# Transposing q and k of a batch with one DMA each, and keeping queries and keys in the same 128-token blocks

## The chip, the core and the metric

The kernel runs on one NeuronCore of one Trainium2 chip. A core has a matrix engine (TensorE, PE in the profile; its weight loads are PEld), a vector engine (VectorE, DVE), a scalar engine (ScalarE, ACT), GpSimd (POOL) and a sync engine (SyncE, SP). POOL and SP are used here mostly to issue DMAs: POOL the loads, which also convert float32 to bfloat16, and SP the transposing DMAs, the stores and a small round trip through DRAM. The transfers of both run on the core's 16 DMA engines. The metric is the device time of one execution in microseconds; lower is better.

## The reference

A sliding-window attention with a distance bias, and behind it a gated feed-forward block. Batch 8, 8 heads, 576 tokens of a sequence, head size 64; the feed-forward block sees 4608 tokens of width 512 and has 1536 hidden channels.

```python
scores = scale * np.matmul(q, k.transpose(0, 1, 3, 2))
rel = pos[:, None] - pos[None, :]
bias = slopes[:, None, None] * (-np.abs(rel).astype(np.float32))[None, :, :]
mask = (rel >= 0) & (rel < 128)
scores = np.where(mask, scores + bias[None], -1000000000.0)
attn = np.exp(scores - np.max(scores, axis=-1, keepdims=True))
attn = attn / (np.sum(attn, axis=-1, keepdims=True) + 1e-09)
x = np.matmul(attn, v)            # then (batch, token, head * 64): 4608 x 512
g, val = x @ w_gate, x @ w_val
out = (0.5 * g * (1.0 + erf(g * inv_sqrt2)) * val) @ w_out
```

## The kernel before

**Attention.** Scores are kept transposed: keys on the partitions, queries along the free dimension. With a window of 128 and keys in blocks of 128, a key block meets at most two blocks of queries, so a head has five score matmuls (`score`, line 130). Key blocks are shifted by 64 tokens: block j holds the keys 128j - 64 to 128j + 63, and the first 64 columns of block 0 are zero padding. Query ranges start at `Q0` and are `NQ` wide: 192, 256, 256, 256 and 128 columns. ScalarE takes the exponential out of PSUM into the tile P (`exp`, line 137), VectorE multiplies with a precomputed mask that holds the bias and the window (`mask`, line 140; the masks `emask` and `emask2` are made once by `masks`). `PCOL` says at which columns of P each key block lies.

Scores need q and k with the head dimension on the partitions. Two heads (a pair c, 0 to 3) share 128 partitions. For batch 0 TensorE transposes them (`transposes`, line 111, through PSUM, and a copy by VectorE, line 116). For all later batches SP issues transposing DMAs (`transposes_dma`, line 122): for one half u of the heads (u = 0: pairs 0 and 1, u = 1: pairs 2 and 3) five for k and five for q, one for each 128 tokens (the fifth has 64), each over 256 columns, that is two blocks of 128 by 128. A batch has twenty of them. `qT` and `kT` exist twice and are used by turns.

**Loads.** `load_qk(b, u)` (line 84) loads half the heads of q and k of a batch with ten DMAs from POOL into slabs `qsb` and `ksb`, which have two buffers each; a slab is free for the next half when its transposes have read it. `load_v(b)` (line 93) loads v in five DMAs with all heads; `load_w` and line 280 load the weights.

**Sums and values.** `sums(b)` (line 191) adds the masked exponentials of all heads with a matmul of ones, VectorE takes the reciprocals (lines 198 and 199), and SP sends them to DRAM (`rd`, line 203) and back as a tile that is spread over all partitions (`rb`, line 205). `values(b, c)` (line 216) is the product with v, and VectorE multiplies by `rb` on the way to `xT` (line 222).

**Feed-forward.** Nine groups g of 512 tokens. `gate_val(g, f)` (line 235) makes a block of 128 hidden channels: eight matmuls, Gelu on ScalarE (line 239), product on VectorE (line 240). `out_half(g, u)` (line 250) is half of the output product of 128 tokens; after every second one ScalarE copies (line 255) and SP stores (line 257).

**Order.** The order of instructions on each engine is the order of the program (a manual schedule): an instruction that waits holds everything behind it on its engine or queue. Ahead of the main loop: loads of batch 0, then of batch 1's first half, v, weights, batch 1's second half; transposes and all eight score steps of batch 0; the transposing DMAs of batch 1's first half; `sums(0)`; the first four score steps of batch 1; `values(0, c)`. Then for each group g: loads and transposing DMAs of a coming batch (group 0: batch 1's second half and batch 2's first; group 1: the rest of batch 2 and batch 3; group g from 2 on: batch g + 2), `load_v(g + 2)`, all of `gate_val` (from group 2 on with `values(g + 1, c)` between), and then score steps and output halves by turns: eight score steps, in group 1 twelve. A batch has eight steps, two for each pair c; from group 2 on they are those of batch g + 2, from pair 0 to pair 3. SP meets the transposing DMAs of a group ahead of that group's stores.

Of the kernel before, what the change touches and what calls it, by code (L numbers as in the profile page):

```python
# [7 lines left out]
FP32 = mybir.dt.float32  # L8
BF16 = mybir.dt.bfloat16
# [5 lines left out]

NQ = (192, 256, 256, 256, 128)
Q0 = (0, 64, 192, 320, 448)

PCOL = (768, 0, 256, 512, 960)
# [5 lines left out]
def kernel(  # L25
# [10 lines left out]
    nc = tc.nc  # L36
    B, H, S, D = q.shape
    W = 128
    NTOK = B * S
    DM = H * D  # L40
# [8 lines left out]
    slab = ctx.enter_context(tc.tile_pool(name="slab", bufs=2))  # L49
# [25 lines left out]
    slabs = {}  # L75

    def load_qk(b, u):

        for nm, src in (("qsb", q), ("ksb", k)):
            t = slab.tile([128, 5, DM // 2], BF16, name=nm)  # L80
            slabs[nm, b, u] = t
            for j in range(5):
                sz = min(128, S - 128 * j)
                nc.gpsimd.dma_start(  # L84
                    out=t[0:sz, j, :].rearrange("p (h d) -> p h d", h=H // 2),
                    in_=src[b][4 * u:4 * u + 4, 128 * j:128 * j + sz, :].rearrange("h p d -> p h d"),
                )

    def load_v(b):
        t = vb[b % 2]  # L90
        for j in range(5):
            lo = 64 if j == 0 else 0
            nc.gpsimd.dma_start(  # L93
                out=t[lo:128, j, :].rearrange("p (h d) -> p h d", h=H),
                in_=v[b][:, 128 * j - 64 + lo:128 * j + 64, :].rearrange("h p d -> p h d"),
            )
# [7 lines left out]
    def transposes(b, c):  # L104
        for nm in ("qsb", "ksb"):
            src = slabs[nm, b, c // 2]
            ps = bank().bitcast(BF16)
            lo = 128 * (c % 2)
            for j in range(5):
                sz = min(128, S - 128 * j)  # L110
                nc.tensor.transpose(
                    out=ps[:, 128 * j:128 * j + sz],
                    in_=src[0:sz, j, lo:lo + 128],
                    identity=ident[0:sz, 0:sz])
            dst = qT[b % 2][:, c, :] if nm == "qsb" else kT[b % 2][:, c, 64:64 + S]
            nc.vector.tensor_copy(out=dst, in_=ps[:, 0:S])

    def transposes_dma(b, u):
        for nm, dst, off in (("ksb", kT[b % 2], 64), ("qsb", qT[b % 2], 0)):
            for j in range(5):  # L120
                sz = min(128, S - 128 * j)
                nc.sync.dma_start_transpose(
                    out=dst[:, 2 * u:2 * u + 2, off + 128 * j:off + 128 * j + sz],
                    in_=slabs[nm, b, u][0:sz, j, :])
# [3 lines left out]
    def score(b, c, i, j, ps, col):  # L128
        lo = 64 * i
        nc.tensor.matmul(  # L130
            out=ps[:, col:col + NQ[j]],
            lhsT=kT[b % 2][lo:lo + 64, c, 128 * j:128 * j + 128],
            rhs=qT[b % 2][lo:lo + 64, c, Q0[j]:Q0[j] + NQ[j]],
            start=True, stop=True)

    def exp(dst, src):
        nc.scalar.activation(out=dst, in_=src, func=AF.Exp, scale=0.125)  # L137
# [26 lines left out]
    def scores2(b, c):  # L164
        P = probs[b, c - c % 2][:, c % 2]
        ps = [bank(), bank()]
        for j in (0, 3):
            for i in (0, 1):
                score(b, c, i, j, ps[i], PCOL[j] - 512)
# [74 lines left out]
    def out_half(g, u):  # L244
# [16 lines left out]
    load_qk(0, 0)  # L261
    relt = consts.tile([128, 256], mybir.dt.int32, name="relt")
    tmpl = consts.tile([128, 256], FP32, name="tmpl")
    nc.gpsimd.affine_select(
        out=ident, in_=ident, compare_op=ALU.not_equal, fill=1.0,
        base=0, pattern=[[-1, 128]], channel_multiplier=1)
    nc.gpsimd.iota(relt, pattern=[[1, 256]], base=0, channel_multiplier=-1)
# [5 lines left out]
    load_qk(0, 1)  # L273
    load_qk(1, 0)
    load_v(0)
    step = DFF // 4
    for n in range(4):
        load_w(step * n, step * (n + 1))
    load_qk(1, 1)
    nc.gpsimd.dma_start(out=wo, in_=moe_w_out.rearrange("(c p) f -> p c f", p=128))  # L280
    load_v(1)
    for i in range(2):
        nc.vector.memset(kT[i][:, :, 0:64], 0.0)
        nc.vector.memset(vb[i][0:64, 0, :], 0.0)
# [4 lines left out]
    nc.vector.memset(emask2[0:64, :, 256:448], 0.0)  # L289

    def masks(c):
# [4 lines left out]
        nc.vector.tensor_copy(out=e2[:, :, 0:256], in_=e)  # L296
        nc.vector.tensor_copy(out=e2[64:128, :, 256:448], in_=e[64:128, :, 64:256])
# [24 lines left out]
    transposes_dma(1, 0)  # L322
# [73 lines left out]
```

## Time and profile before

| | |
|---|---|
| median of 3 runs | 456.78 us (454.81 to 457.54) |
| profiled execution | 456.34 us |
| its span, first to last instruction | 454.6 us |
| TensorE busy (weight loads beside it) | 368.8 us, 81% (167.0 us) |
| VectorE, ScalarE, GpSimd busy | 184.4, 176.3, 157.6 us |
| mean granted TensorE clock | 0.935 |
| DMA packets, bytes | 166000, 46.61 MB, 151568 of them under 512 B |
| DMA queue of POOL's loads | 119568 packets, 18.89 MB, 57.8% of 16 engines' span |
| DMA queue of SP | 46400 packets, 27.30 MB, 26.4% |

Times in rows of the profile count from the start of the span. A row of the timeline has start, length, engine, line, operation, output and inputs with shapes, how many instructions are merged in it, and in brackets how long the engine had been idle before it and what ended that. SPq is SP's queue of DMA issues: the length is the time that SP spends on issuing, not that of the transfer. "Landing" is the time from the issue to the end of the transfer. A row of the windows has the window, its length, the busy time of each engine with its number of instructions, the granted clock, the share of time in which the DMA engines were busy (it can be above 1, since transfers of several queues overlap) and GB/s.

### The profile page before, as it was taken

The page shows a single profiled execution, that of the slowest core. Times are in us where ns is not written, and L with a number is a line of the kernel's source. Part 1 is how long each engine was busy: PE and PEld are TensorE (multiplying, and loading weights), DVE is VectorE, ACT ScalarE, POOL GpSimd, SP SyncE. Part 2 cuts the span into 40 slices and gives each one's busy share as a digit, 9 for nine tenths or more (in the row PEclk, how much of TensorE's full clock was granted, in tenths as well). Part 3 has the DMA queues.
Part 4 walks back from the last instruction along what each step waited for, and adds up shares of the span by engine and source line. Part 5 has one row for each costly group of instructions (what it writes and reads, how often), then busy time and mean ns, then how long its engine had stood idle before and what let it go on. Part 6 is the DMA issues. An engine that isn't in the chain of part 4 may idle for free. (4 is left out here: it accounts for less than half of the span.)

```text
span 454.6 us, 6481 instructions
## 1 busy us (share of the span) xinstructions
PE 368.8 (81%) x2424; PEld 167.0 (37%) x2424; DVE 184.4 (41%) x281; ACT 176.3 (39%) x326; POOL 157.6 (35%) x218
## 2 busy tenths in 40 slices
PE   2631399749978569969995999689968999999996
PEld 1220234314434134423442344234423444444442
DVE  2481344615345074434453355325542651230330
ACT  1350423524364314364435442544254422332321
POOL 8993173951095640249024900681000000000000
PEclk9999889859997689998999799989997999999999
DMA  8999999999199999499949994999521321101002
GB/s 52 78 128 174 228 139 161 132 146 176 41 96 125 133 169 163 62 105 128 162 65 106 118 125 96 97 126 142 96 47 71 80 50 48 46 0 71 24 1 93
DMA packets 166000, 46.61 MB, mean 103 GB/s; under 512 B 151568, under 2 KB 157200, under 8 KB 165968
## 3 DMA queue, kind: packets, MB, share of 16 engines
q0 software_dynamic: 119568, 18.89, 57.8%
q1 hardware_dynamic: 46400, 27.30, 26.4%
q8 instruction: 19, 0.31, 0.3%
q14 instruction: 13, 0.11, 0.1%
HBM read 47.19 MB, written 9.58 MB: 125 GB/s over the span
## 5 line engine op out<-in xcount | busy, mean ns | idle before, releaser
L240 DVE TENSOR_TENSOR hT<-ps,gelu 128x512 bf16<-128x512 f32 x108 | 74.7, 691 | 124.2 <-PE ps L235 124.1
L235 PE MATMUL ps<-xT,wg 128*128 128x512 bf16 x432 | 112.4, 382 | 7.8 <-DVE xT L222 7.4
L250 PE MATMUL ps<-wo,hT 128*128 128x512 bf16 x432 | 115.1, 416 | 0.1
L239 ACT ACTIVATE gelu<-ps 128x512 bf16<-128x512 f32 x108 | 64.5, 597 | 126.3 <-PE ps L235 125.9
L235 PE MATMUL ps<-xT,wv 128*128 128x512 bf16 x432 | 111.6, 381 | 0.0
L84 POOL DMA_DIRECT2D qsb<-in_q_dram x80 | 58.0, 754 | 131.5 <-DMA qT<-qsb 113.2
L137 ACT ACTIVATE P<-ps 128x512 bf16<-128x512 f32 (+2 forms) x160 | 72.9, 553 | 69.1 <-PE ps L130 69.0
L140 DVE TENSOR_TENSOR P<-P,emask 128x1024 bf16<-128x1024 bf16 x64 | 46.1, 724 | 88.1 <-ACT P L137 88.1
L130 PE MATMUL ps<-qT,kT 64*128 64x256 bf16 (+2 forms) x320 | 29.6, 304 | 45.4 <-DMA qT<-qsb 42.6
L84 POOL DMA_DIRECT2D ksb<-in_k_dram x80 | 58.3, 781 | 18.4 <-DMA qsb<-in_q_dram 9.3
L235 PEld LDWEIGHTS <-wg 128*128 128x128 bf16 x432 | 41.1, 98 | 58.1 <-issue 8.9
L250 PEld LDWEIGHTS <-hT 128*128 128x128 bf16 x432 | 41.3, 104 | 57.4 <-issue 22.5
L235 PEld LDWEIGHTS <-wv 128*128 128x128 bf16 x432 | 42.4, 98 | 52.0 <-issue 1.5
L255 ACT COPY osb<-ps 128x512 f32<-128x512 f32 x36 | 21.2, 588 | 69.8 <-PE ps L250 52.4
L130 PEld LDWEIGHTS <-kT 64*128 64x128 bf16 x320 | 12.9, 105 | 68.2 <-issue 56.5
L222 DVE TENSOR_TENSOR xT<-ps,rb 128x320 bf16<-128x320 f32 x64 | 25.4, 449 | 24.7 <-DMA rb<-rd 23.7
L93 POOL DMA_DIRECT2D vb<-in_v_dram x40 | 34.2, 933 | 0.5 <-DMA qsb<-in_q_dram 0.5
L191 PE MATMUL ps<-P,ones 128*32 128x128 bf16 (+2 forms) x384 | 14.5, 281 | 13.9 <-DVE P L140 13.7
L216 PE MATMUL ps<-P,vb 128*64 128x128 bf16 (+2 forms) x384 | 20.8, 248 | 1.4 <-DVE xT L222 1.4
L198 DVE RECIPROCAL r<-ps 128x320 f32<-128x320 f32 x8 | 17.3, 2157 | 6.2 <-PE ps L191 6.2
L216 PEld LDWEIGHTS <-vb 128*64 128x64 bf16 x384 | 15.0, 111 | 11.9 <-issue 11.7
L191 PEld LDWEIGHTS <-ones 128*32 128x32 bf16 x384 | 10.9, 111 | 18.5 <-issue 18.2
(31 smaller groups left out, 68.8 us busy)
## 6 DMA issues: line engine op xcount, KB each, us to landing
rb<-rd SPq DMA_DIRECT2D x16, 576.0 KB, 6.0
out_dram<-osb SPq DMA_DIRECT2D x36, 256.0 KB, 2.7
qsb<-in_q_dram POOLq DMA_DIRECT2D x64, 64.0 KB, 3.2
ksb<-in_k_dram POOLq DMA_DIRECT2D x64, 64.0 KB, 3.5
vb<-in_v_dram POOLq DMA_DIRECT2D x32, 128.0 KB, 5.0
wg<-in_moe_w_gate_dram POOLq DMA_DIRECT2D x4, 384.0 KB, 12.9
wv<-in_moe_w_val_dram POOLq DMA_DIRECT2D x4, 384.0 KB, 14.3
wo<-in_moe_w_out_dram POOLq DMA_DIRECT2D x1, 1536.0 KB, 14.3
```

The costliest lines, as they stand in the source:

```text
L84: nc.gpsimd.dma_start(out=t[0:sz, j, :].rearrange("p (h d) -> p h d", h=H // 2), in_=src[b][4 * u:4 * u + 4, 128 * j:128 * j + sz, :].rear ...
L93: nc.gpsimd.dma_start(out=t[lo:128, j, :].rearrange("p (h d) -> p h d", h=H), in_=v[b][:, 128 * j - 64 + lo:128 * j + 64, :].rearrange("h ...
L130: nc.tensor.matmul(out=ps[:, col:col + NQ[j]], lhsT=kT[b % 2][lo:lo + 64, c, 128 * j:128 * j + 128], rhs=qT[b % 2][lo:lo + 64, c, Q0[j]:Q0 ...
L137: nc.scalar.activation(out=dst, in_=src, func=AF.Exp, scale=0.125)
L140: nc.vector.tensor_tensor(out=dst, in0=dst, in1=m, op=ALU.mult)
L191: nc.tensor.matmul(out=ps[s][32 * c:32 * c + 32, a - QS * s:e - QS * s], lhsT=ones[:, i, :], rhs=probs[b, c - c % 2][:, c % 2, i, col:col ...
L216: nc.tensor.matmul(out=ps[s][64 * i:64 * i + 64, a - QS * s:e - QS * s], lhsT=vb[b % 2][:, j, 64 * h:64 * h + 64], rhs=P[:, i, col:col + e ...
L222: nc.vector.tensor_tensor(out=xT[:, c, b * S + lo:b * S + hi], in0=ps[s][:, 0:hi - lo], in1=recip[b][:, c, lo:hi], op=ALU.mult)
L235: nc.tensor.matmul(out=ps, lhsT=w[:, c, 128 * f:128 * (f + 1)], rhs=xT[:, c, t0:t0 + 512], start=(c == 0), stop=(c == 3))
L239: nc.scalar.activation(out=gl, in_=pg, func=AF.Gelu)
L240: nc.vector.tensor_tensor(out=hid[g][:, f, :], in0=pv, in1=gl, op=ALU.mult)
L250: nc.tensor.matmul(out=po, lhsT=hid[g][:, f, 128 * t:128 * (t + 1)], rhs=wo[:, f, :], start=(f == 0), stop=(f == NF - 1))
```

## The change

q and k of a batch are loaded whole, all eight heads in five DMAs each, in the same shifted token blocks as v (the first block holds 64 tokens, its other 64 rows are zero), into one buffer `qs` and one `ks`. Each is then transposed by one DMA over all of its 20 blocks of 128 by 128, instead of ten. `qT` and `kT` get the form (block, pair, token). Because queries now lie in the same blocks as keys, key block j is scored against the query blocks j and j + 1; block 0 scores 256 columns instead of 192, the first 64 of which are padding that the exponential leaves out. The columns of P and the masks move accordingly.

The order changes too. Batch 0 is loaded whole at once, after the identity is made. The loads of batch 1, v and the weights stand behind the score steps of batch 0 in the program, and batch 1 is loaded and transposed whole there. In the loop, group g loads and transposes batch g + 2, in groups 0 and 1 as in all others.

```diff
-PCOL = (768, 0, 256, 512, 960)
+PCOL = (512, 0, 256, 704, 960)
...
-    slab = ctx.enter_context(tc.tile_pool(name="slab", bufs=2))
...
-    qT = [consts.tile([128, 4, S], BF16, name=f"qT{i}") for i in range(2)]
-    kT = [consts.tile([128, 4, 64 + S], BF16, name=f"kT{i}") for i in range(2)]
+    qs, ks = (consts.tile([128, 5, DM], BF16, name=f"{nm}s") for nm in "qk")
+    qT, kT = ([consts.tile([128, 5, 4, 128], BF16, name=f"{nm}T{i}") for i in range(2)]
+              for nm in "qk")
...
-    def load_v(b):
-        t = vb[b % 2]
+    def load(t, src, b):
         for j in range(5):
             lo = 64 if j == 0 else 0
             nc.gpsimd.dma_start(
                 out=t[lo:128, j, :].rearrange("p (h d) -> p h d", h=H),
...
+    def load_qk(b):
+        load(qs, q, b)
+        load(ks, k, b)
+
+    def load_v(b):
+        load(vb[b % 2], v, b)
...
-    def transposes_dma(b, u):
-        for nm, dst, off in (("ksb", kT[b % 2], 64), ("qsb", qT[b % 2], 0)):
-            for j in range(5):
-                sz = min(128, S - 128 * j)
-                nc.sync.dma_start_transpose(
-                    out=dst[:, 2 * u:2 * u + 2, off + 128 * j:off + 128 * j + sz],
-                    in_=slabs[nm, b, u][0:sz, j, :])
+    def transposes_dma(b):
+        for src, dst in ((ks, kT), (qs, qT)):
+            nc.sync.dma_start_transpose(
+                out=dst[b % 2].rearrange("p j c t -> p (j c) t"),
+                in_=src.rearrange("p j x -> p (j x)"))
...
     def score(b, c, i, j, ps, col):
         lo = 64 * i
+        n = 1 if j == 4 else 2
         nc.tensor.matmul(
-            out=ps[:, col:col + NQ[j]],
-            lhsT=kT[b % 2][lo:lo + 64, c, 128 * j:128 * j + 128],
-            rhs=qT[b % 2][lo:lo + 64, c, Q0[j]:Q0[j] + NQ[j]],
+            out=ps[:, col:col + 128 * n].rearrange("p (n t) -> p n t", n=n),
+            lhsT=kT[b % 2][lo:lo + 64, j, c, :],
+            rhs=qT[b % 2][lo:lo + 64, j:j + n, c, :],
...
-            exp(P[:, i, 512:960], ps[i][:, 0:448])
+            exp(P[:, i, 512:960], ps[i][:, 64:512])
...
-    load_qk(0, 0)
...
+    load_qk(0)
...
-    load_qk(0, 1)
-    load_qk(1, 0)
-    load_v(0)
-    step = DFF // 4
-    for n in range(4):
-        load_w(step * n, step * (n + 1))
-    load_qk(1, 1)
-    nc.gpsimd.dma_start(out=wo, in_=moe_w_out.rearrange("(c p) f -> p c f", p=128))
-    load_v(1)
...
-    transposes_dma(1, 0)
+    load_qk(1)
+    load_v(0)
+    step = DFF // 4
+    for n in range(4):
+        load_w(step * n, step * (n + 1))
+    nc.gpsimd.dma_start(out=wo, in_=moe_w_out.rearrange("(c p) f -> p c f", p=128))
+    load_v(1)
+    transposes_dma(1)
     sums(0)
...
-    LOADS = {0: ((1, 1), (2, 0)), 1: ((2, 1), (3, 0), (3, 1))}
+    def fetch(b):
+        if b < B:
+            load_qk(b)
+            transposes_dma(b)
+
     for g in range(NG):
         late = g < 2
-        for b, u in LOADS.get(g, ((g + 2, 0), (g + 2, 1))):
-            if b < B:
-                if (b, u) != (1, 1):
-                    load_qk(b, u)
-                transposes_dma(b, u)
+        fetch(g + 2)
```

More of the change, by code (lines that the diff above doesn't have):

```diff
@@ L260 @@
     nc.vector.memset(ident, 0.0)
-    load_qk(0, 0)
-    relt = consts.tile([128, 256], mybir.dt.int32, name="relt")
-    tmpl = consts.tile([128, 256], FP32, name="tmpl")
+    for t in (qs, ks):
+        nc.vector.memset(t[0:64, 0, :], 0.0)
     nc.gpsimd.affine_select(
@@ L266 @@
         base=0, pattern=[[-1, 128]], channel_multiplier=1)
+    load_qk(0)
+    relt = consts.tile([128, 256], mybir.dt.int32, name="relt")
+    tmpl = consts.tile([128, 256], FP32, name="tmpl")
     nc.gpsimd.iota(relt, pattern=[[1, 256]], base=0, channel_multiplier=-1)
@@ L288 @@
         nc.vector.memset(ones[:, i, 16 * i:16 * i + 16], 1.0)
[L289 removed]
+    nc.vector.memset(emask2[0:64, :, 0:192], 0.0)
     def masks(c):
```

36 lines of the change are left out of this document (10 added, 26 removed).

## The prediction

> **What bounds the kernel now.** I read the costliest groups of the page first: which idle time stands in front of TensorE's work, and what ended it.
>
> ```profile
> L130 PE MATMUL ps<-qT,kT 64*128 64x256 bf16 (+2 forms) x320 | 29.6, 304 | 45.4 <-DMA qT<-qsb 42.6
> ```
>
> In front of the score matmuls TensorE idles 45.4 us, and 42.6 of them end when a transpose of q lands. No other idle time of TensorE is near that. Next the windows, cut at the gate/value phases and at the phases behind them in which scores and output alternate (group 0's, group 1's, then those of groups 2 to 5, with one gate/value phase between as a measure). The columns are length, then busy time of PE, PEld, DVE, ACT and POOL with counts, granted clock, DMA share, GB/s.
>
> ```profile
> 79.90:109.40 29.50, 20.59 (x186) 9.01 (x186) 12.77 (x18) 11.68 (x24) 19.92 (x27) 0.77 1.57 156
> ...
> 130.20:170.30 40.10, 26.59 (x253) 13.09 (x253) 18.35 (x25) 16.20 (x34) 25.44 (x34) 0.79 1.38 136
> ...
> 193.80:215.00 21.20, 16.71 (x140) 6.79 (x137) 8.43 (x12) 11.06 (x24) 14.51 (x20) 0.92 1.16 116
> 215.00:238.50 23.50, 23.50 (x145) 10.79 (x143) 12.44 (x20) 9.75 (x15) 3.14 (x5) 1.00 0.78 115
> 238.50:262.00 23.50, 17.99 (x140) 7.08 (x137) 8.46 (x12) 11.08 (x24) 15.72 (x22) 0.85 1.14 112
> ...
> 285.50:308.00 22.50, 16.52 (x140) 6.82 (x137) 8.42 (x12) 11.06 (x24) 16.70 (x24) 0.92 1.18 117
> ...
> 331.50:354.30 22.80, 17.79 (x140) 7.08 (x137) 8.44 (x12) 11.09 (x24) 0.00 (x0) 0.85 0.18 55
> ```
>
> The gate/value phase is full (23.50 of 23.50 at clock 1.00). The score phases are not: five microseconds idle and a clock below 1. The four of groups 2 to 5 last 21.2 + 23.5 + 22.5 + 22.8 = 90.0 us; groups 0 and 1 have 29.5 and 40.1. These 159.6 us are where the change can act; what follows 354.3 has no attention but the last values, and is full. Now TensorE, then SP's queue, around group 3's score phase (start, length, what, and in brackets the idle time before it):
>
> ```profile
> 238.52 0.69 PE L130 MATMUL ps<-qT,kT 64*128 64x128 bf16 x12
> ...
> 249.15 0.82 PE L130 MATMUL ps<-qT,kT 64*128 64x128 bf16 x8 [5.02 <-DMA qT<-qsb]
> 249.90 2.74 PE L250 MATMUL ps<-wo,hT 128*128 128x512 bf16 x6
> ...
> 258.95 0.26 PE L191 MATMUL ps<-P,ones 128*32 128x192 bf16 x3
> 259.67 1.10 PE L191 MATMUL ps<-P,ones 128*32 128x192 bf16 x45 [0.46 <-DVE P L140]
> 260.70 1.47 PE L250 MATMUL ps<-wo,hT 128*128 128x512 bf16 x6
> ```
>
> ```profile
> 220.39 0.55 SPq L257 DMA_DIRECT2D out_dram<-osb  x1
> 221.05 6.49 SPq L122 DMA_TRANSPOSE kT<-ksb  x5
> 227.59 6.38 SPq L122 DMA_TRANSPOSE qT<-qsb  x5
> 234.08 7.39 SPq L122 DMA_TRANSPOSE kT<-ksb  x5
> 241.52 6.38 SPq L122 DMA_TRANSPOSE qT<-qsb  x5
> ```
>
> SP issues twenty transposes one behind the other from 221.05 to 247.90, 26.8 us. Those of heads 4 to 7 are out only at the end, and TensorE, which has used up heads 0 to 3 at 249.15 - 5.02 = 244.13, waits for them. So the bound of a score phase is SP's issue time, not the moving of the bytes:
>
> ```profile
> 229.00:233.00 4.00, 4.00 (x29) 1.82 (x27) 2.11 (x4) 1.07 (x2) 0.00 (x0) 1.00 0.27 60
> ```
>
> Here SP issues transposes without a gap and the DMA engines are 27% busy.
>
> **The price of a long transpose.** An instruction of now covers 2 blocks of 128 columns; one of the change covers 20. No such instruction is in the trace. A full block row (128 tokens), a short one (64 tokens), and the landing times:
>
> ```profile
> L122 SPq DMA_TRANSPOSE qT<-qsb x1: 1189/1189/1189, 231.5 to 231.5; - x1
> ```
>
> ```profile
> L122 SPq DMA_TRANSPOSE qT<-qsb x1: 1158/1158/1158, 232.8 to 232.8; - x1
> ```
>
> ```profile
> DMA to landing us min/median/max: 2.3/2.4/7.4
> ```
>
> Half the tokens cost the same, so rows are not what SP pays for; it pays for the instruction, for column blocks, or both. Lower end: all fixed, 1.2 us. Upper end: all by blocks, 20 / 2 x 1.19 = 11.9 us. SP's plain DMA of 0.55 us, quoted above, is the nearest row to a fixed part alone; with 0.55 fixed a block costs (1.19 - 0.55) / 2 = 0.32 and the long one 0.55 + 20 x 0.32 = 6.95 us. I take 7.0, two of them 14.0 instead of 26.8. The bytes: 0.27 x 1.28 = 0.35 us of all engines per instruction now, 3.5 us for ten, hidden under the issue.
>
> The Trainium skill, page "DMA: Bandwidth & Descriptors", table of sequencer cycles, column for previous generations, speaks against any saving by the tile: 8,192 tiles take 262,144 cycles, so 32 for each, however many stand in one instruction. With tiles of 16 rows by 128 (the xbar tile of the page's section "DMA Transpose (X-bar)") and SP at 1.2 GHz ("Trainium Kernel Development and Optimization", NeuronCore Architecture), 160 tiles would take 4.3 us, an instruction some 5, and the sum would be some 4 us less, an estimate. The equal rows for 64 and 128 tokens do not agree with a cost by 16-row tiles.
>
> **Groups 2 to 5.** SP comes to the transposes at 221.05 as now (the stores, reciprocals and their DMAs before them are untouched), so q is on its way at 235.05 and landed at 237.45, 1.1 us ahead of the first score at 238.52. The wait goes, and the slow clock behind it. What is left: the first half phase is 244.13 - 238.52 = 5.6 us, the second has the same work less four small matmuls, 5.6; from the sums (258.95) to the phase's end (262.00) 3.1 us, 0.46 of them waiting for the last mask. Without the pause ScalarE and VectorE have no time to catch up, so this wait grows; the nearest other row for it is group 0's, 2.10 us:
>
> ```profile
> 86.78 1.10 PE L191 MATMUL ps<-P,ones 128*32 128x192 bf16 x45 [2.10 <-DVE P L140]
> 87.80 2.59 PE L250 MATMUL ps<-wo,hT 128*128 128x512 bf16 x6
> ```
>
> I take 1.3 more, between 0 and 2.1: 5.6 + 5.6 + 3.1 + 1.3 = 15.6 us, four times 62.4 instead of 90.0: -27.6 us. If the clock falls behind this wait as it does here, where six output matmuls take 2.59 instead of 1.47, each group pays 1.1 more, 4.5 in all; I leave it out because nothing of the kind follows the 0.46 (1.47 at 260.70).
>
> On this the Trainium skill, "TensorE: Matmul & The Clock Gate", Part 1, says that the half clock comes after about 3.4 us without work. By it these waits cost no clock; the 2.59 after 2.10 us of waiting does not agree with it, and by that row the total is the 4.5 us later.
>
> **The start.** POOL loads full-width blocks: one such DMA takes 4.39 / 5 = 0.88 us against 0.75 for half the heads,
>
> ```profile
> 1.26 3.74 POOL L84 DMA_DIRECT2D qsb<-in_q_dram  x5 [0.82 <-POOLq L380]
> ...
> 24.82 4.39 POOL L93 DMA_DIRECT2D vb<-in_v_dram  x5
> ```
>
> so batch 0 is issued by 1.3 + 0.4 (the identity, now first) + 10 x 0.88 = 10.5 and landed at some 13.5. But batch 1 goes into the same buffers, so POOL waits until TensorE has transposed the last heads of batch 0, which stand behind two steps of scores: at about 18 (estimate). Behind that wait stand the loads of batch 1, v, all weights: batch 1 is issued by 27 (v began at 24.82) and landed at 31. Then SP:
>
> ```profile
> 30.72 7.76 SPq L122 DMA_TRANSPOSE qT<-qsb  x5
> 38.58 0.70 SPq L203 DMA_DIRECT2D rd<-r  x1
> 44.19 1.32 SPq L205 DMA_DIRECT2D rb<-rd  x2
> ...
> 81.36 6.31 SPq L122 DMA_TRANSPOSE kT<-ksb  x5
> ```
>
> ```profile
> 55.83 1.55 DVE L222 TENSOR_TENSOR xT<-ps,rb 128x320 bf16<-128x320 f32 x4 [6.15 <-DMA rb<-rd]
> ```
>
> The reciprocals of batch 0 go through DRAM behind the transposes on SP (38.58), come back at 55.8, and the first gate matmul follows. With two long transposes from 31 that DMA leaves at 45.0, 6.4 later, and gate/value of group 0 starts 6.4 later. Bounds: 2.6 earlier (short price) to 11 later (long price); the transposes meet the weights, which the waits of 44.19 to 55.83 hold already.
>
> **Groups 0 and 1.** Up to batch 2's keys the loads carry as many rows as now (the second half of its heads comes in, v of batch 2 goes behind), from 2.2 us later: 81.36 becomes 83.5, and q lands at 83.5 + 14.0 + 2.4 = 99.9, where TensorE now gets its piece at 97.01:
>
> ```profile
> 97.01 0.82 PE L130 MATMUL ps<-qT,kT 64*128 64x128 bf16 x8 [6.61 <-DMA qT<-qsb]
> ```
>
> The rest of the phase is as now: group 1 begins 2.9 late, +2.9 for everything up to there. In group 1 three sets of transposes become one, which waits for nothing in this phase:
>
> ```profile
> 150.37 0.62 SPq L203 DMA_DIRECT2D rd<-r  x1
> ```
>
> ```profile
> 152.49 0.82 PE L130 MATMUL ps<-qT,kT 64*128 64x128 bf16 x8 [5.16 <-DMA qT<-qsb]
> ```
>
> ```profile
> 136.57 1.97 PE L191 MATMUL ps<-P,ones 128*32 128x192 bf16 x45 [1.61 <-DVE P L140]
> ```
>
> ```profile
> 137.72 2.16 DVE L198 RECIPROCAL r<-ps 128x320 f32<-128x320 f32 x1 [1.21 <-PE ps L191]
> ...
> 162.22 1.55 DVE L222 TENSOR_TENSOR xT<-ps,rb 128x320 bf16<-128x320 f32 x4 [13.94 <-DMA rb<-rd]
> ```
>
> The wait of 5.16 goes, and the reciprocals of batch 2 no longer stand behind transposes until 150.37. What is late next is their way through DRAM, now 162.22 - 150.37 = 11.9 us. Sums end 138.54 - 130.20 = 8.3 us into the phase; the two reciprocals, 2.16 and by its 256 columns 1.73, end at 137.72 + 3.9 = 141.6, 11.4 into it; the way back ends at 23.3; the last products, sums and output are some 5.2 more (estimate): 28.5 us instead of 40.1, -11.6 (between -8 and -13).
>
> **Small things.** Block 0 now scores 256 columns instead of 192:
>
> ```profile
> L130 PE MATMUL ps<-qT,kT 64*128 64x256 bf16 x192 | 24.9, 324 | 0.5 <-ACT P L137 0.5
> ...
> L130 PE MATMUL ps<-qT,kT 64*128 64x192 bf16 x64 | 9.5, 286 | 0.0
> ```
>
> 64 x 38 ns = 2.4 us, partly in waits: +2. Half as many load instructions on POOL buy nothing in the later groups, where POOL has time. That waits go by the parts of a tile really touched is assumed; without it the start is some us longer.
>
> **Sum.** Span 454.6, profiled execution 456.34 (1.74 around the span), median of the runs 456.78, 0.44 above. 456.34 + 2.9 - 11.6 - 27.6 + 2 = 422.0 us.
>
> **Rivals.** *Near-fixed price* (1.2 to 3 us): for it, that half the tokens cost nothing less. The start is 2.6 earlier, group 0's phase is limited by its reciprocals (-6.2), group 1 -13, the four phases -29, +2: 407. *Late loads*: one buffer for q and one for k, so the next batch loads only when q has landed. The loop is 14.0 + 2.4 + 8.8 + some 4 landing = 29 us against 23.5 + 15.6 = 39 for a group, so it needs landings 10 us longer; landings of up to 7.4 speak for some of it. With phases 3.8 us longer it gives 437. *The one instruction costs what the ten cost* (slower): at 11.9 us q lands at 221.05 + 23.8 + 2.4 = 247.25, and now no heads at all are ready at 238.52: 8.7 us of waiting, 2.5 of slow clock (2.74 for 1.47, twice), 0.8 of the mask's wait saved, a phase of 26, four of them +14; the start shifts group 1 by 83.5 + 26.2 - 97.01 = 12.7; 12.7 - 11.6 + 14 + 2 = +17: 473. A group begins to wait above 7.5 us, and the kernel is slower above some 10.3. Against it: a fixed part must then be nearly nothing, and SP's shortest quoted DMA takes 0.55. For it: twenty blocks may fill a queue that two do not.
>
> **Numbers.** Main case 0.55 (410 to 432), near-fixed price 0.13, late loads 0.14, slower rival 0.18, of which 0.04 ends within 1%. A difference of 1% is about what can be told from no change. Faster 0.82, same 0.04, slower 0.14. The range runs from the near-fixed case to past late loads: 406 to 446.
>
> **What would show it.** SP with two transposes of 5 to 7 us per batch; no row of score matmuls waiting for qT from 170 on and granted clock near 1 in those phases, each 15 to 17 us long; the first gate matmul at 60 to 64. Wrong if the long transposes last over 7.5 us, if their landing trails the issue by much more than 2.4, or if keys of the next batch are still loading when SP reaches them.

## The result, and the profile after

| | before | changed |
|---|---|---|
| median | 456.50 us (454.81 to 457.54) | 427.19 us (424.62 to 431.19) |
| ratio, 95% interval | | 0.9343 [0.9287, 0.9398] |
| second series, unchanged kernel again | 457.02 us | 430.44 us (428.26 to 431.23), 0.9424 [0.9379, 0.9469] |

The changed kernel takes 6 to 7% less time. The profile taken with the first series is its longest execution (431.19 us), which its ratio leaves out because it lies more than 1.5% above the fastest; the profile of the second series (431.02 us, span 429.2) shows the same starts of the groups within 2.2 us, and the rows here are its own. What makes other executions of the same kernel 3 to 7 us shorter no profile shows.

From the costliest groups, the row of the score matmuls:

```profile
L119 PE MATMUL ps<-qT,kT 64*128 64x256 bf16 (+1 forms) x320 | 26.9, 278 | 34.9 <-DMA qT<-qs 31.6
```

There are still 31.6 us of waiting for q, against 42.6. But it is another wait. The windows (length, busy time of PE, PEld, DVE, ACT and POOL, granted clock, DMA share, GB/s), first the start, then the score phases of groups 0 to 5:

```profile
36.00:50.00 14.00, 0.00 (x0) 0.00 (x0) 0.00 (x0) 0.00 (x0) 2.05 (x3) 0.50 1.41 128
...
98.80:123.80 25.00, 18.26 (x182) 8.61 (x185) 13.23 (x19) 11.62 (x24) 11.06 (x14) 0.95 1.22 137
145.20:172.70 27.50, 21.73 (x250) 10.88 (x254) 16.75 (x24) 15.91 (x34) 4.19 (x5) 0.94 0.43 83
196.20:211.80 15.60, 14.79 (x136) 6.41 (x138) 8.45 (x12) 11.03 (x24) 9.95 (x12) 1.00 1.86 162
...
235.30:250.90 15.60, 14.79 (x136) 6.42 (x138) 8.44 (x12) 11.03 (x24) 7.13 (x9) 1.00 1.51 138
274.40:290.00 15.60, 14.79 (x136) 6.42 (x138) 8.44 (x12) 11.02 (x24) 6.88 (x9) 1.00 1.49 138
313.50:329.10 15.60, 14.79 (x136) 6.42 (x138) 8.44 (x12) 11.02 (x24) 0.00 (x0) 1.00 0.14 51
```

The four phases of groups 2 to 5 last 15.60 us each, 62.4 instead of 90.0, at clock 1.00. In the start there are 14 us in which TensorE, VectorE and ScalarE do nothing while the DMA engines are fully taken (a share of 1.41); POOL only issues three loads. TensorE around group 3's phase and in the start (start, length, what, idle time before it and what ended that):

```profile
61.46 2.10 PE L119 MATMUL ps<-qT,kT 64*128 64x128 bf16 x20 [31.61 <-DMA qT<-qs]
63.49 3.65 PE L205 MATMUL ps<-P,vb 128*64 128x192 bf16 x48
74.66 2.77 PE L224 MATMUL ps<-xT,wg 128*128 128x512 bf16 x4 [7.51 <-DMA wo<-in_moe_w_out_dram]
...
105.63 1.10 PE L180 MATMUL ps<-P,ones 128*32 128x192 bf16 x45 [2.10 <-DVE P L129]
106.66 1.47 PE L239 MATMUL ps<-wo,hT 128*128 128x512 bf16 x5
...
121.00 0.41 PE L205 MATMUL ps<-P,vb 128*64 128x128 bf16 x6 [4.09 <-DVE xT L211]
...
235.28 0.72 PE L119 MATMUL ps<-qT,kT 64*128 64x128 bf16 x12
...
248.55 1.10 PE L180 MATMUL ps<-P,ones 128*32 128x192 bf16 x45 [0.43 <-DVE P L129]
```

All of the wait for q is the one of 31.61 us ahead of batch 1's first scores. The next wait is put down to `wo`, but the gate matmul needs xT, and that came with the reciprocals:

```profile
73.78 3.00 DVE L211 TENSOR_TENSOR xT<-ps,rb 128x320 bf16<-128x320 f32 x8 [6.76 <-DMA rb<-rd]
```

SP's queue of DMA issues, in the start, in group 0 and in group 3:

```profile
30.53 5.73 SPq L110 DMA_TRANSPOSE kT<-ks  x1
36.39 15.47 SPq L110 DMA_TRANSPOSE qT<-qs  x1
51.91 0.71 SPq L192 DMA_DIRECT2D rd<-r  x1
61.54 1.31 SPq L194 DMA_DIRECT2D rb<-rd  x2
88.47 4.14 SPq L110 DMA_TRANSPOSE kT<-ks  x1
92.72 2.78 SPq L110 DMA_TRANSPOSE qT<-qs  x1
...
215.79 1.26 SPq L194 DMA_DIRECT2D rb<-rd  x2
217.14 0.56 SPq L246 DMA_DIRECT2D out_dram<-osb  x1
217.93 6.71 SPq L110 DMA_TRANSPOSE kT<-ks  x1
224.83 2.69 SPq L110 DMA_TRANSPOSE qT<-qs  x1
```

In group 3 both transposes are out at 227.5, 9.6 us after the first began, against 26.8 for twenty, and 7.8 us ahead of the scores of 235.28. In the start the one of q holds SP for 15.47 us. The reciprocals leave behind it, at 51.91, and are in DRAM only at 61.54 (when their way back begins), just as q lands.

Where the 25.3 us between the two profiled executions (456.34 and 431.02) come from, by the first gate matmul of each group:

| stage | before | changed | difference | predicted |
|---|---|---|---|---|
| up to group 0 | 56.7 | 74.7 | +18.0 | +6.4 |
| group 0 | 52.7 | 49.2 | -3.5 | -3.5 |
| group 1 | 60.9 | 48.8 | -12.1 | -11.6 |
| groups 2 to 5 | 184.0 | 156.4 | -27.6 | -27.6 |
| the rest | 100.2 | 100.1 | -0.1 | 0 |
| small things | | | | +2 |

### The profile page after: what moved, and what is told of

Read it like the earlier page. It is cut to its first block, busy times and chain, and to the rows that moved or that the text cites. A ratio compares the mean times of both kernels' runs of the same rounds, so it can differ in the third digit from the quotient of the medians.

```text
span 429.4 us, 6083 instructions
## 1 busy us (share of the span) xinstructions
PE 352.6 (82%) x2385; PEld 164.5 (38%) x2424; DVE 183.6 (43%) x281; ACT 176.0 (41%) x326; POOL 109.6 (26%) x138
## 5 line engine op out<-in xcount | busy, mean ns | idle before, releaser
L229 DVE TENSOR_TENSOR hT<-ps,gelu 128x512 bf16<-128x512 f32 x108 | 74.7, 691 | 126.4 <-PE ps L224 126.3
L224 PE MATMUL ps<-xT,wg 128*128 128x512 bf16 x431 | 114.1, 386 | 7.7 <-DMA wo<-in_moe_w_out_dram 6.9
L224 PE MATMUL ps<-xT,wv 128*128 128x512 bf16 x415 | 110.4, 384 | 0.7 <-issue 0.2
L239 PE MATMUL ps<-wo,hT 128*128 128x512 bf16 x411 | 99.8, 382 | 2.6 <-issue 1.9
L80 POOL DMA_DIRECT2D qs<-in_q_dram x40 | 33.7, 859 | 113.7 <-DMA qT<-qs 93.5
L239 PEld LDWEIGHTS <-hT 128*128 128x128 bf16 x432 | 38.7, 98 | 49.6 <-issue 9.4
L119 PE MATMUL ps<-qT,kT 64*128 64x256 bf16 (+1 forms) x320 | 27.4, 284 | 33.8 <-DMA qT<-qs 30.2
L244 ACT COPY osb<-ps 128x512 f32<-128x512 f32 x36 | 21.2, 588 | 63.2 <-PE ps L239 41.6
L80 POOL DMA_DIRECT2D ks<-in_k_dram x40 | 33.8, 897 | 0.0
L119 PEld LDWEIGHTS <-kT 64*128 64x128 bf16 x320 | 11.7, 101 | 53.2 <-issue 47.8
L205 PE MATMUL ps<-P,vb 128*64 128x128 bf16 (+2 forms) x384 | 21.7, 259 | 3.7 <-DVE xT L211 3.7
L205 PEld LDWEIGHTS <-vb 128*64 128x64 bf16 x384 | 16.0, 117 | 14.1 <-issue 13.8
```

Source lines behind the costliest of these rows:

```text
L80: nc.gpsimd.dma_start(out=t[lo:128, j, :].rearrange("p (h d) -> p h d", h=H), in_=src[b][:, 128 * j - 64 + lo:128 * j + 64, :].rearrange(" ...
L119: nc.tensor.matmul(out=ps[:, col:col + 128 * n].rearrange("p (n t) -> p n t", n=n), lhsT=kT[b % 2][lo:lo + 64, j, c, :], rhs=qT[b % 2][lo: ...
L205: nc.tensor.matmul(out=ps[s][64 * i:64 * i + 64, a - QS * s:e - QS * s], lhsT=vb[b % 2][:, j, 64 * h:64 * h + 64], rhs=P[:, i, col:col + e ...
L224: nc.tensor.matmul(out=ps, lhsT=w[:, c, 128 * f:128 * (f + 1)], rhs=xT[:, c, t0:t0 + 512], start=(c == 0), stop=(c == 3))
L229: nc.vector.tensor_tensor(out=hid[g][:, f, :], in0=pv, in1=gl, op=ALU.mult)
L239: nc.tensor.matmul(out=po, lhsT=hid[g][:, f, 128 * t:128 * (t + 1)], rhs=wo[:, f, :], start=(f == 0), stop=(f == NF - 1))
```

## The experiments

**Theories.** The groups went as predicted; the start is 18 us later instead of 6.4. *Collision* (the weights theory of the expectations): the long transposes run beside the bulk loads of v and weights, which slow them and hold the reciprocals behind them on SP. *Single buffer* (their buffer theory): batch 1 can be loaded only when batch 0 has been transposed, and this sets the start. *The form of the transposes* (price by instruction or by block) is what the groups gain by. All ratios are to the kernel before on the same chip. The table first; gate 0, 1 and 2 are the first gate matmul of groups 0, 1 and 2 in the profile.

| run | median us | ratio, 95% interval | gate 0 | gate 1 | gate 2 |
|---|---|---|---|---|---|
| e1_pe_b1 | 412.34 | 0.9051 [0.8999, 0.9103] | 51.9 | 105.5 | 156.7 |
| e2_pieces2 | 469.69 | 1.033 [1.027, 1.039] | 75.3 | 127.5 | 182.2 |
| e3_w_wait | 413.58 | 0.9079 [0.9029, 0.9128] | 51.7 | 104.4 | 153.2 |
| e4_two_bufs | 425.88 | 0.9345 [0.9285, 0.9405] | 66.9 | 116.2 | 165.2 |
| e0_after | 430.44 | 0.9424 [0.9379, 0.9469] | 74.7 | 123.8 | 172.7 |
| e5_pieces4 | 431.27 | 0.9450 [0.9394, 0.9506] | 69.9 | 119.5 | 168.6 |
| e6_order | 414.41 | 0.9090 [0.9044, 0.9135] | 51.2 | 105.9 | 154.8 |
| e7_pe_order | 412.34 | 0.9011 [0.8956, 0.9067] | 51.8 | 103.3 | 154.7 |
| e8_start_wait | 419.81 | 0.9204 [0.9135, 0.9273] | 62.0 | 114.8 | 164.7 |
| e9_start_nowait | 422.09 | 0.9272 [0.9197, 0.9347] | 60.8 | 113.7 | 163.4 |
| e11_w0_first | 417.33 | 0.9143 [0.9085, 0.9200] | 55.4 | 108.3 | 157.4 |
| e10_pe_w0_first | 411.52 | 0.8986 [0.8935, 0.9038] | 46.7 | 100.0 | 149.6 |

**Batch 1 by TensorE (e1_pe_b1).** One part undone: batch 1 is transposed by TensorE, which stands idle then; single buffer and loads stay.

```diff
-    transposes_dma(1)
     sums(0)
+    transposes(1, 0)
+    transposes(1, 1)
     for n in range(4):
         todo.pop(0)[1]()
+        if n in (0, 2):
+            transposes(1, 2 + n // 2)
```

> The changed kernel with one part undone: batch 1 is transposed by TensorE and copied by VectorE, as batch 0 is, and SP issues no transpose before batch 2. Weights theory (the start is late because the long transpose of q, 14.72 us on SP, shares the DMA engines with the weights, and the DMA of the reciprocals stands behind it): scores of batch 1 at 34 to 37 instead of 60.3, the reciprocals leave SP at 34 instead of 50.8, first gate matmul at 52 to 57 instead of 73.1, total 406 to 411. Buffer theory (the start is late because POOL idles 7.0 us until TensorE has read the one buffer, and v and the weights stand behind that): the first gate matmul stays within 3 us of 73, total 424 to 428.

Measured 412.34 us. The queue of SP:

```profile
32.83 0.70 SPq L192 DMA_DIRECT2D rd<-r  x1
38.83 1.31 SPq L194 DMA_DIRECT2D rb<-rd  x2
```

With no transpose before them the reciprocals leave at 32.83 instead of 51.91, and the gate begins at 51.86 instead of 74.66, with the same single buffer and the same loads. So what the start loses beyond the prediction goes with the transposes on SP and not with the late loading, of which the prediction had counted its part. Of these 22.8 us 16.3 are left at the end of the span: in group 0 TensorE now waits 8.55 us for xT instead of 4.09, and group 1 is 2.4 us longer. The median is 1.3 us above the range given for this theory.

**Twenty pieces (e2_pieces2).** All other parts of the change kept, only the transposes cut into pieces of two blocks as before.

```diff
-        for src, dst in ((ks, kT), (qs, qT)):
-            nc.sync.dma_start_transpose(
-                out=dst[b % 2].rearrange("p j c t -> p (j c) t"),
-                in_=src.rearrange("p j x -> p (j x)"))
+        for u in range(2):
+            for src, dst in ((ks, kT), (qs, qT)):
+                for j in range(5):
+                    nc.sync.dma_start_transpose(
+                        out=dst[b % 2][:, j, 2 * u:2 * u + 2, :],
+                        in_=src[:, j, 256 * u:256 * u + 256])
```

> The changed kernel with the transposes of batches 1 to 7 cut into pieces of 2 blocks again, twenty for a batch, in the old order (heads 0 to 3 of k and q, then heads 4 to 7); layout, loads and buffers stay. If the gain of groups 2 to 5 comes from fewer instructions on SP: a piece takes 1.19 us on SP, the wait of 4 to 5.5 us for qT is back in each of the four score phases with the slow clock behind it, the phases are 21 to 23.5 us instead of 15.6, total 450 to 458. If it comes from the loads or the layout: phases stay at 15.6 to 17, total 425 to 432.

Measured 469.69 us, slower than before and 11.7 us above the range given for it; groups 0 and 1 are 3.0 and 5.9 us longer than in the change too, which I had not counted. The windows of the four phases, and SP in one of them:

```profile
205.70:227.10 21.40, 16.50 (x138) 6.75 (x138) 8.48 (x12) 11.12 (x24) 12.56 (x15) 0.92 1.32 126
250.60:274.40 23.80, 17.71 (x136) 7.06 (x138) 8.45 (x12) 11.08 (x24) 12.57 (x15) 0.86 1.29 124
297.90:322.40 24.50, 17.49 (x136) 7.01 (x138) 8.44 (x12) 11.07 (x24) 12.56 (x15) 0.86 1.27 122
345.90:367.80 21.90, 16.42 (x135) 6.69 (x137) 8.40 (x12) 11.03 (x24) 0.00 (x0) 0.92 0.20 61
```

```profile
233.11 6.49 SPq L112 DMA_TRANSPOSE kT<-ks  x5
239.66 6.39 SPq L112 DMA_TRANSPOSE qT<-qs  x5
246.14 6.92 SPq L112 DMA_TRANSPOSE kT<-ks  x5
253.10 6.40 SPq L112 DMA_TRANSPOSE qT<-qs  x5
```

21.4 + 23.8 + 24.5 + 21.9 = 91.6 us, as the 90.0 before, with the low clock. With layout, loads and buffers of the change kept, what groups 2 to 5 gain is gone: it hangs on the transposes being few. The rest of the change, without that, costs 3.3%: what it costs lies in the start (gate 0 at 75.3 instead of 56.7).

**Weights behind the transposes (e3_w_wait).** The transposing DMAs stay on SP, but POOL issues weights, `wo` and v of batch 1 only when q of batch 1 has landed: it reads 16 columns of it first.

```diff
+    transposes_dma(1)
+    seen = consts.tile([128, 16], BF16, name="seen")
+    nc.gpsimd.tensor_copy(out=seen, in_=qT[1][:, 0, 0, 0:16])
     step = DFF // 4
     for n in range(4):
...
-    transposes_dma(1)
     sums(0)
```

> The changed kernel with one wait added on POOL: the weights and v of batch 1 are issued only when q of batch 1 has been transposed (POOL reads 16 columns of it first). Weights theory: unhindered, the long transposes take 2.7 us (q) and 3 to 5 us (k) on SP, q has landed by 42 instead of 60.3, the reciprocals come back by 50, first gate matmul at 53 to 60; later gate blocks may wait some us for their weights; total 408 to 417. Buffer theory: the weights come 9 us later than now and the first gate matmul moves back with them to about 80, total 432 to 436.

Measured 413.58 us. The queue of SP:

```profile
29.92 5.25 SPq L110 DMA_TRANSPOSE kT<-ks  x1
35.29 2.82 SPq L110 DMA_TRANSPOSE qT<-qs  x1
38.16 0.71 SPq L192 DMA_DIRECT2D rd<-r  x1
40.40 1.31 SPq L194 DMA_DIRECT2D rb<-rd  x2
```

The same transpose of q takes 2.82 instead of 15.47 us, and the reciprocals' way into DRAM 2.2 instead of 9.6. The gate begins at 51.7 although the weights leave 9 us later. That is the collision, shown by taking away the other party, the weights. What it costs is paid in group 0, where q of batch 2, loaded behind `wo`, is late. TensorE's row there:

```profile
92.24 0.82 PE L119 MATMUL ps<-qT,kT 64*128 64x128 bf16 x8 [6.92 <-DMA qT<-qs]
```

**Two buffers (e4_two_bufs).** `qs` and `ks` exist twice.

```diff
-    qs, ks = (consts.tile([128, 5, DM], BF16, name=f"{nm}s") for nm in "qk")
+    qs, ks = ([consts.tile([128, 5, DM], BF16, name=f"{nm}s{i}") for i in range(2)]
+              for nm in "qk")
...
-        load(qs, q, b)
-        load(ks, k, b)
+        load(qs[b % 2], q, b)
+        load(ks[b % 2], k, b)
...
```

> The changed kernel with two buffers each for q and k of a batch, used by turns, so that POOL loads batch 1 without waiting for TensorE. Weights theory: loads, transposes and weights all come 7 us earlier and meet as before; the long transpose of q still takes over 8 us on SP; first gate matmul at 64 to 68, total 418 to 423. Buffer theory: the transposes get ahead of the weights and take under 5 us, first gate matmul below 60, total 407 to 414. In groups 2 to 5 neither expects a change (15.6 us a phase).

Measured 425.88 us. The queue of SP:

```profile
23.56 5.03 SPq L111 DMA_TRANSPOSE kT<-ks  x1
28.71 15.84 SPq L111 DMA_TRANSPOSE qT<-qs  x1
```

Everything comes 7 us earlier, and the weights with it, so q's transpose takes 15.84 us again and the start is 7.8 us better, no more. The start is where the collision put it, the total some 3 us above what was then expected. The ratio lies between the two of the change: a second buffer alone is worth little.

**The change again (e0_after).** Unchanged, for the spread and the second profile shown above.

> The changed kernel once more, beside the others on one chip, for a second profile of its start: median 424 to 429; score phases of groups 2 to 5 at 15.6 us as in its first profile; the long transpose of q of batch 1 again over 10 us on SP.

Measured 430.44 us, 1.4 above the range given for it, the spread 428.26 to 431.23; the first series had 424.62 to 431.19.

**Ten pieces of four blocks (e5_pieces4).** One instruction for each 128 tokens with all heads, ten for a batch.

```diff
-            nc.sync.dma_start_transpose(
-                out=dst[b % 2].rearrange("p j c t -> p (j c) t"),
-                in_=src.rearrange("p j x -> p (j x)"))
+            for j in range(5):
+                nc.sync.dma_start_transpose(
+                    out=dst[b % 2][:, j, :, :],
+                    in_=src[:, j, :])
```

> The changed kernel with the transposes of batches 1 to 7 cut by token block: pieces of 4 blocks, ten for a batch. It tells what SP pays for. The prediction's price (0.55 us and 0.32 a block): 1.83 us a piece, q landed 6 + 18.3 + 2.4 = 26.7 us into a group, 3 us of waiting and the slow clock in each of the four phases, total 440 to 450. A price by the two unhindered lengths seen (1.19 us for 2 blocks, 2.70 for 20, so 1.02 and 0.084 a block): 1.36 us a piece, q landed just in time, phases 15.6 to 17, total 425 to 436. A price by the instruction alone: 1.19 us.

Measured 431.27 us, from two executions. The tile view of q, durations in ns as least, median and longest, here and then in the change:

```profile
L111 SPq DMA_TRANSPOSE qT<-qs x35: 1210/1225/4295, 34.5 to 309.9; - x35
```

```profile
L110 SPq DMA_TRANSPOSE qT<-qs x7: 2659/2697/15467, 36.4 to 303.1; - x7
DMA to landing us min/median/max: 4.3/4.3/4.5
```

Four blocks take 1.21 us where two took 1.19: up to there SP pays for the instruction. Twenty blocks take 2.66 and not 6, and there the DMA engines are full: while SP issues the one for q, in the change from 224.83 to 227.52, their share is 1.22 at 278 GB/s, and in e6, from 37.70 to 38.50 and with little else under way, 1.28 at 291 GB/s; beside the pieces of two before it was 0.27 at 60 GB/s. The transfer goes on after SP is free (2.7 us on SP, 4.3 to landing). So at twenty blocks the moving of the bytes is the limit, as far as these windows show it. Ten instructions for a batch are nearly enough as well: with the waits for q ahead of them (0.86 and 2.04 us, in groups 3 and 4) the phases of groups 2 to 5 last 15.6, 16.4, 19.2 and 15.6 us.

**Better orders for the start (e6_order, e7_pe_order).** e6 is e3 with v of batch 0 and the first quarter of the weights loaded while POOL waits for TensorE, and q and k of batch 2 loaded ahead of `wo`. e7 is e1 with the same orders, without POOL's wait.

```diff
     load_qk(0)
...
+    load_v(0)
+    step = DFF // 4
+    load_w(0, step)
...
     load_qk(1)
-    load_v(0)
-    step = DFF // 4
-    for n in range(4):
+    transposes_dma(1)                                   # e6 only
...
+    nc.gpsimd.tensor_copy(out=seen, in_=qT[1][:, 0, 0, 0:16])   # e6 only
+    for n in range(1, 4):
         load_w(step * n, step * (n + 1))
+    load_qk(2)
     nc.gpsimd.dma_start(out=wo, in_=moe_w_out.rearrange("(c p) f -> p c f", p=128))
...
-            load_qk(b)
+            if b != 2:
+                load_qk(b)
```

> The kernel with the wait on POOL ahead of the weights, and its loads reordered: v of batch 0 and the first quarter of the weights go out in the 7 us in which POOL waits for TensorE, and q and k of batch 2 ahead of the output weights. Weights theory: q of batch 1 still takes under 4 us on SP, the first gate matmul is at 47 to 51, the wait of 6.9 us for q of batch 2 shrinks to under 3, total 403 to 410. If the loads of batch 1 are slowed by what now runs beside them, first gate matmul at 51 to 55 and total 410 to 414.

> Batch 1 transposed by TensorE, and the same reordering of the loads, without a wait on POOL. Weights theory: reciprocals leave SP at 33 as in the run with TensorE's transposes, but meet the weights on their way; first gate matmul at 47 to 52; the wait of 8.6 us for the reciprocals of batch 1 in group 0 shrinks, since fewer loads stand behind; total 402 to 410. If that wait stays: 409 to 413.

Measured 414.41 and 412.34 us. The queue of SP in e6:

```profile
32.40 2.59 SPq L110 DMA_TRANSPOSE kT<-ks  x1
35.11 2.60 SPq L110 DMA_TRANSPOSE qT<-qs  x1
...
67.58 8.03 SPq L110 DMA_TRANSPOSE kT<-ks  x1
75.73 7.55 SPq L110 DMA_TRANSPOSE qT<-qs  x1
```

With no load under way k and q cost the same, 2.6 us: the price with nothing beside it. With `wo` and others under way the next pair costs 8.0 and 7.6, so the wait for q in group 0 only falls from 6.92 to 3.61. In e7 group 1 begins at 103.3 after a wait of 5.73 for xT. e7 lies within its second range, e6 0.4 us above its own. Neither is told apart from e3 and e1 by the intervals.

**Loads earlier, weights held or not (e8_start_wait, e9_start_nowait).** Two buffers; loads in the order q and k of batches 0 and 1, v, a quarter of the weights, q and k of batch 2; then the rest of the weights, `wo` and v. In e8 POOL first waits for the reciprocals' way back (it reads 16 columns of `rb`), in e9 not.

```diff
     load_qk(1)
     load_v(0)
     step = DFF // 4
+    load_w(0, step)
+    transposes_dma(1)
+    load_qk(2)
+    sums(0)
...
+    nc.gpsimd.tensor_copy(out=seen, in_=recip[0][:, 0, 0:16])   # e8 only
-    for n in range(4):
+    for n in range(1, 4):
...
-    transposes_dma(1)
-    sums(0)
...
-            load_qk(b)
+            if b != 2:
+                load_qk(b)
```

> Two buffers each for q and k, and the start ordered by what is needed first: q and k of batches 0 and 1, v of batch 0, the first quarter of the weights, q and k of batch 2; then POOL waits until the reciprocals of batch 0 are back from DRAM, and only then come the rest of the weights, the output weights and v of batch 1. Weights theory: the long transposes of batch 1 take under 6 us each on SP and end by 35, the reciprocals leave at 34 and are back by 44, since no weights are under way; first gate matmul at 44 to 48 instead of 73.1; q of batch 2 is there in time, group 1 at 88 to 96; total 394 to 404. If the loads of batch 2 (packets of 256 B) are as bad a neighbour as the weights: first gate matmul at 50 to 56, total 404 to 414.

> The same without POOL's wait for the reciprocals: the rest of the weights follows q and k of batch 2 at once, from some 35 us. Weights theory: the transposes are past by then, but the reciprocals' way through DRAM meets the weights, 10 to 12 us for the way back as in the runs before; first gate matmul at 49 to 54, total 400 to 410.

Measured 419.81 and 422.09 us: both missed. The queue of SP in e8:

```profile
23.47 5.75 SPq L111 DMA_TRANSPOSE kT<-ks  x1
29.34 15.27 SPq L111 DMA_TRANSPOSE qT<-qs  x1
```

I had counted the first quarter of the weights as small. It leaves at 24.2 to 25.7, right beside the transposes, and with the loads of batch 2 behind it q's transpose takes 15.27 us as in the change. In e9 it takes 13.17, and batch 2's pair, beside the other weights, 10.30 and 17.21. A quarter of the weights is enough for most of the harm, as e11 shows next.

**The first quarter ahead (e11_w0_first, e10_pe_w0_first).** e11 is e8 with that quarter right behind batch 0's loads, so that only q, k and v are loaded beside the transposes. e10 is e11 with batch 1 transposed by TensorE, by the edit of e1. Against e8:

```diff
     load_qk(0)
...
+    step = DFF // 4
+    load_w(0, step)
...
     load_v(0)
-    step = DFF // 4
-    load_w(0, step)
     transposes_dma(1)
     load_qk(2)
```

> As the kernel with two buffers and POOL's wait for the reciprocals, but the first quarter of the weights goes out right after batch 0, so that beside the transposes of batch 1 only loads of q, k and v (256 B packets) are under way, and no weights. Weights theory: then q of batch 1 takes under 5 us on SP (it took 15.3 with a quarter of the weights beside), first gate matmul at 44 to 49, total 395 to 405. Any-load theory (a long transpose is slowed by whatever POOL's loads have under way): q still takes over 9 us on SP, first gate matmul at 54 to 62, total 412 to 421.

> The same loads with batch 1 transposed by TensorE instead, so that no transposing DMA is issued before batch 2's. Both theories: reciprocals leave at 33 and meet loads of q and k only; first gate matmul at 44 to 50; the transposes of batch 2 run beside the weights and take over 8 us each, but have 25 us; group 1 starts at 93 to 100 instead of 103 to 105 in the other runs with TensorE's transposes; total 398 to 408. If the reciprocals are held up by the loads as by weights: first gate matmul at 51 to 54, total 406 to 413.

Measured 417.33 and 411.52 us. The queue of SP in e11, and TensorE in e10, the first gate matmul and two waits of group 2:

```profile
26.48 4.45 SPq L111 DMA_TRANSPOSE kT<-ks  x1
31.05 8.74 SPq L111 DMA_TRANSPOSE qT<-qs  x1
39.85 0.70 SPq L193 DMA_DIRECT2D rd<-r  x1
45.81 1.31 SPq L195 DMA_DIRECT2D rb<-rd  x2
```

```profile
46.67 2.77 PE L225 MATMUL ps<-xT,wg 128*128 128x512 bf16 x4 [5.86 <-DVE xT L212]
...
167.51 1.02 PE L225 MATMUL ps<-xT,wv 128*128 128x512 bf16 x4 [1.64 <-DVE xT L212]
...
177.24 1.22 PE L120 MATMUL ps<-qT,kT 64*128 64x128 bf16 x12 [2.24 <-DMA qT<-qs]
```

Beside the loads of v, q and k alone the transpose takes 8.74 us, between the 2.6 with nothing under way and the 13 to 17 with weights, which is between what the two theories said; time and gate of e11 lie in the ranges given for harm by any load. In e10 the gate begins 5.2 us earlier than in e1 and group 2 7.1 earlier, but group 2 then lasts 44.8 instead of 39.1: it waits for xT (1.64) and for q (2.24), so most of the gain is gone, and the total is 3.5 us above the first range given.

This goes with the two buffers: group 2 lasts 39.1 us in the change, e1, e3, e6 and e7, and 39.8 to 44.8 in all five kernels that have two. In e4 q and k of a later batch are loaded from 164.66 on, beside the reciprocals and transposes of group 2 (k's takes 9.99 us), in the change from 193.58 on, behind them (7.27); that this is the reason no run separates.

e10 has the lowest ratio, 10.1% below the kernel before. The intervals of e1, e3 and e7 overlap with its own, that of e6 lies just above it. All five are faster than both the change and the kernel before; e1 and e3 are the smallest edits.

## Why the prediction was right, and where not

**Sign and size: right.** 422.0 was predicted, with 406 to 446 around it; 427.19 is the median and 431.02 the profiled execution, with which the sum is to be compared: 9.0 us more. By the table of stages 11.6 of it come up to group 1's start (+14.5 instead of +2.9), -0.5 from group 1, -0.1 from the end, and -2 because the small things did not show.

**Groups 2 to 5: -27.6 and -27.6, by two errors that cancel.** The wait for q and the low clock go, as said. But the phase was built as 5.6 + 5.6 + 3.1 + 1.3 = 15.6 us, and its parts are otherwise, though it is 15.60 in all four. The 1.3 for a longer wait at the sums did not come (0.43 us at 248.55, as before). The second half phase lasts 7.0 us, from 240.84 to the sums at 247.85, and not 5.6: it holds four of the output halves, the first three, at 1.4 us each. That the sum is exact is luck. e2 shows that it is the instructions: with twenty the phases are 91.6 us.

**The clock behind a wait.** The 1.1 us for each group that I left out did not appear: groups 2 to 5 are at clock 1.00. Behind the longer wait of group 0 it is open. The row of before had 2.59 for six output matmuls after 2.10 us of waiting; in the change the same 2.10 at 105.63 is followed by matmuls at 1.47 (106.66), but in e8 (93.46) by 2.74, and in group 1 of the change waits of 1.41 and 1.61 are followed by 2.34 for five (153.26). By the Trainium skill, "TensorE: Matmul & The Clock Gate", Part 1, the half clock comes after an idle window of about 3.4 us. The row of 106.66 agrees with that if each wait is taken by itself, those of before, of e8 and of 153.26 do not, and what decides between them no run shows.

**The price of a long transpose: mis-sized.** "0.55 fixed and 0.32 per block" gave 7.0 us. Undisturbed it is 2.6, near the low end of 1.2 to 11.9. The step that failed is the division of 1.19 us into a part for the issue and a part for blocks: e5's row, 1.21 for four blocks, shows no part for blocks there. The other step is "3.5 us for ten, hidden under the issue": with 2.6 us of issue the bytes are no longer hidden but the limit, by the windows given with e5. The near-fixed rival had the right price, though not because it is fixed. That the main case's total was nevertheless the nearer one comes from the start. In the groups k's transpose takes 6.7 us where the way back of the reciprocals left SP just before (215.79, then 217.93), so the pair was 9.6 instead of 14.0; all of it hidden, as anything below 7.5 each was said to be. By the Trainium skill, "DMA: Bandwidth & Descriptors", table of sequencer cycles, 32 cycles a tile gave an estimate of 4.3 us for 160 tiles of 16 rows by 128. Measured were 2.6 us, so with tiles of that size the rule does not hold here.

**The start: wrong.** The sentence that failed is "the transposes meet the weights, which the waits of 44.19 to 55.83 hold already". Those 11.6 us were the reciprocals' way back alone; the transposes ahead of them, one half of batch 1, were out by 38.58. The change puts twice the bytes onto SP ahead of the reciprocals, in the time in which the weights are loaded. The transposes took 5.73 + 15.47 = 21.2 us instead of 14.0, the reciprocals' way into DRAM 9.6 us, and only then the 12 us of the way back began, which I had counted: +18.0 instead of +6.4, outside the bounds of -2.6 to +11. The upper bound was too low as well: two transposes at the upper price of 11.9 would have let the reciprocals leave at 31 + 23.8 = 54.8, 16.2 later than 38.58. Of the 11.6 us beyond the prediction 6.9 are lost on SP (51.91 instead of 45.0), 4.0 on the way into DRAM (9.6 instead of 5.6, which it took before) and 0.6 on the way back. e3 takes away the weights and e1 the transposes; in both the gate begins at 51.7 to 51.9. Batch 1 was late as said (POOL waited until 18.48 for TensorE, expected at about 18), and e4 shows what that alone is worth: 7.8 us.

**Group 0: right for another reason.** I had its phase wait for q of batch 2 until 99.9. It landed at about 97 (92.72 and the 4.3 of the tile view), ahead of the phase, which began only at 98.80. In place of that wait stands one of 4.09 us for xT (121.00), behind the reciprocals of batch 1. From gate to gate 49.2 us, and 49.2 by my steps; the agreement is chance.

**Group 1: right, -12.1 against -11.6.** Its phase is 27.50 us, 28.5 was said, with the round trip of the reciprocals as the next limit; TensorE waits for xT nowhere in this phase any more, so that round trip is not its limit.

**The rivals.** Late loads did not come: in group 3 the pair is under way 6.1 us behind the first gate matmul, before it was 6.0, and SP reaches it without a wait. The slower rival needed a price above 10.3 us; it is met only beside the weights, once, in the start, where it costs 11.6 us more than said. e2 is near in time to what was worked out for one instruction that costs what the pieces do, 469.69 us and 473, but by chance: there +14 were to come from groups 2 to 5, and e2 has +1.6 there and +18.6 in the start.

## What to carry to other kernels

A queue that issues many small transposes can be the bound though the DMA engines idle: one large instruction in place of ten cut 12.8 us of issue (q of one batch) to 2.7. But such a transfer fills the DMA engines, is slowed several times by bulk loads beside it, and holds its queue all that time, so look at what is loaded then, and at the short round trip behind it on which the next stage waits. Where the matrix engine idles anyway, in the start, it can do the same transposes (e1); holding the weights back did as well here (e3).

## What the runs showed that I had not expected

- The transpose of 20 blocks holds SP for 2.6 us with nothing under way (e6), 8.7 beside loads of q, k and v (e11), 7.3 to 7.6 beside `wo` and v (e6, e7), 13 to 17 beside the gate and value weights (the change, e4, e8, e9). In the pieces of e5 the five of q took 13.33 us in the start against 6.5 in group 3, so that it is not the length of the instruction that makes it sensitive.
- A DMA of 18 KB behind it took 9.6 us to reach DRAM in the change and 2.2 in e3; beside the weights, but with no transpose ahead of it, it took 6.0 (e1).
- Two or four blocks, 64 or 128 tokens cost SP the same: 1.16 to 1.23 us.
- A second buffer can hurt: in e4 later transposes run beside loads that the single buffer had held back (6.47 us for q of batch 2, 2.78 in the change), and group 2 lasts 40.4 us instead of 39.1.
